# Top-k attention and a cosine-gated layer on one core: weights decoded 2**8 times as large, their sign put in by VectorE

## The chip, the core and the metric

The kernel runs on one core of a Trainium2 chip. The core has a matrix engine (TensorE, PE in the profile), three engines for elementwise work (VectorE or DVE, ScalarE or ACT, GpSimd or POOL), a queue that only issues transfers (SyncE, SP), and 16 DMA engines. Each engine works through its own instructions in the order of the program and waits on semaphores for the others. The metric is the time of one execution on the device in microseconds (us). The kernel before takes 1515.18 us, the median of five runs (1513.1 to 1517.51).

## The reference, cut to what matters

```python
# q, k, v: (8, 8, 576, 64); w_in: (512, 2048); w_out: (2048, 512)
scores = 1.0 / np.sqrt(D) * np.matmul(q, k.transpose(0, 1, 3, 2))
kth = np.partition(scores, -32, axis=-1)[..., -32:-31]
scores = np.where(scores >= kth, scores, -1000000000.0)
scores = scores - np.max(scores, axis=-1, keepdims=True)
attn = np.exp(scores)
attn = attn / (np.sum(attn, axis=-1, keepdims=True) + 1e-09)
x = np.matmul(attn, v).transpose(0, 2, 1, 3).reshape(4608, 512)
h = x @ w_in
out = ((h * np.cos(h)) @ w_out).astype(np.float32)
```

The two weight matrices reach the kernel as 64-bit floating point numbers. No engine here computes on these, so the kernel reads each one as two 32-bit words (`lo`, `hi`) and makes a 32-bit float of them: this is the decoding that the change is about. The high word holds the sign, 11 bits of exponent and 20 bits of mantissa.

## The kernel before

The 4608 rows are cut into 36 blocks of 128, and each block is worked on for two heads at a time, which makes 144 units. The main loop (L775) goes through slots, one for each unit and one more. In slot i VectorE searches the 32 largest scores of unit i: `topk_first` begins with the folds (L244, on the scores that ScalarE copied from PSUM in `take_scores`, L230 and L231), and four rounds of searches follow (L304, L307). ScalarE, a slot behind, masks and exponentiates unit i-1 (`bounds`, `mask`, `exponentials`, L314 to L339) and ends with `den`, the sum of the exponentials. VectorE takes its reciprocal (L343), GpSimd multiplies by it (`normalise`, L348), PE transposes the result and multiplies it by v (`values`, L408), and ScalarE copies the product into xT (L414).

There are three kinds of slots. In the `early_slot` (0 to 8) the transposes are made by PE (`transposes_now`, L382, with copies by ScalarE in L386 and L389) within the same slot, and the reciprocal waits for the exponentials of this slot. In the `slot` (9 to 140) GpSimd rearranges the halves of each word (`split`, L360), and two DMAs on SP's queue write them to memory and bring them back transposed, two slots later. The `last_slot` is again like the early one.

Between these the matrix products of the second part are fed to PE in small portions (`feed`): `ff1` (L465, xT with w_in, taken out by ScalarE in `take_first`, L478) and `ff2` (L543, with w_out, taken out in `take_second`, L553). The cosine needs a reduction to one period, on GpSimd in L504 to L513 (`reduce_first`, `reduce_second`), a sine on ScalarE (L523) and a product on GpSimd (`gate`, L530). How many portions a slot may feed is counted while the program is built, with a credit of some five for each slot, and a product is fed only when its weights were decoded a slot before. So the order of each engine's instructions is fixed in the program.

The weights come in 32 chunks of 128 x 512, 16 of w_in and 16 of w_out. Up to eight staging tiles `st` (they share their memory with the tiles g) are filled by DMAs on SP's queue (`load_weights`). Each chunk is then decoded in three steps, by three engines:

- `decode_first`, ScalarE, three passes: the magnitude of the high word, read as a float and multiplied by 2**16 (L126); the sign of the high word as +1 or -1, written over it (L127); the low word multiplied by 2**-29, which leaves the three bits that are still wanted (L128).
- `decode_second`, VectorE, two operations: a maximum with 2.0, which keeps small values out of the way (L137), and a shift of the bits to the left by 3, which drops the surplus bits of the exponent (L138).
- `decode_third`, GpSimd, two operations: the three low bits are added as integers (L147), and the float is multiplied by the sign (L148).

Slots 0 to 5 decode three chunks in their `decode_second`, slots 6 to 12 two. In the early slots `decode_second` stands ahead of the reciprocal, and `decode_third` behind `normalise`; ScalarE's `decode_first` stands in part ahead of the copies L386, in part behind them. In slots 9 to 12 `decode_second` comes right after `topk_first`, and `decode_third` stands behind `normalise`, `split` and `gate` and ahead of the reduction.

Of the kernel before, what the change touches and what calls it, by code (L numbers as in the profile page):

```python
# [10 lines left out]
F32 = mybir.dt.float32  # L11
# [3 lines left out]
AF = mybir.ActivationFunctionType  # L15
ALU = mybir.AluOpType
# [9 lines left out]
INV_2PI = 1.0 / (2.0 * math.pi)  # L26
# [5 lines left out]
def kernel(  # L32
# [9 lines left out]
    nc = tc.nc  # L42
# [32 lines left out]
    DECODE = moe_w_in.dtype != F32  # L75
# [9 lines left out]
    for i in range(DF // CW):  # L85
        w = consts.tile([P, NC, CW], F32, tag=f"w_in{i}", name=f"w_in{i}")
# [4 lines left out]
    for f in range(NF):  # L91
        w = consts.tile([P, DM], F32, tag=f"w_out{f}", name=f"w_out{f}")
# [10 lines left out]
    def load_weights(n):  # L103
        for _ in range(n):
# [12 lines left out]
            wq["loaded"].append((st, dst))  # L117
            wq["next"] = i + 1

    def decode_first(n):  # L120


        for _ in range(min(n, len(wq["loaded"]))):
            st, w = wq["loaded"].popleft()
            lo, hi = st[:, :, 0], st[:, :, 1]
            nc.scalar.activation(out=w, in_=hi.bitcast(F32), func=AF.Abs, scale=2.0**16)  # L126
            nc.scalar.sign(hi.bitcast(F32), hi)  # L127
            nc.scalar.mul(out=lo, in_=lo.bitcast(U32), mul=2.0**-29)  # L128
            wq["second"].append((st, w))

    def decode_second(n):


        for _ in range(min(n, len(wq["second"]))):
            st, w = wq["second"].popleft()
            wi = w.bitcast(I32)
            nc.vector.tensor_scalar(out=w, in0=w, scalar1=2.0, scalar2=None, op0=ALU.max)  # L137
            nc.vector.tensor_scalar(  # L138
                out=wi, in0=wi, scalar1=3, scalar2=None, op0=ALU.logical_shift_left
            )  # L140
            wq["third"].append((st, w))

    def decode_third():
        while wq["third"]:
            st, w = wq["third"].popleft()
            wi = w.bitcast(I32)
            nc.gpsimd.tensor_tensor(out=wi, in0=wi, in1=st[:, :, 0], op=ALU.add)  # L147
            nc.gpsimd.tensor_tensor(out=w, in0=w, in1=st[:, :, 1].bitcast(F32), op=ALU.mult)  # L148
            wq["done"] += 1


# [298 lines left out]
    def ff1(blk, i):  # L450
        w = blk["w"]
        nf = 256 // w
        part = i % 4
        if part == 0:
            blk["g"].append(ffw.tile([P, 1024], F32, tag="g", name="g", bufs=CHUNKS))
            ff["live"] += 1
        if part % 2 == 0:
            open_bank()
            blk["mm"] = ps.tile([P, 512], F32, tag="mm", name="mm", bufs=2)
        g, mm = blk["g"][-1], blk["mm"]  # L460
        for a in range(nf):
            f = i * nf + a
            at = (part % 2 * nf + a) * w
            for c in range(NC):
                nc.tensor.matmul(  # L465
                    mm[:, at : at + w],
                    w_in[f // FC][:, c, (f % FC) * P : (f % FC + 1) * P],
                    blk["xT"][:, c],
                    start=c == 0,
                    stop=c == NC - 1,  # L470
                )
        if part % 2 == 0:
            return
        ff["open"] -= 1
        full.append((take_first, blk, g, mm, part // 2))

    def take_first(blk, g, mm, half):
        nc.scalar.mul(out=g[:, half * 512 : half * 512 + 512], in_=mm, mul=INV_2PI)  # L478
        if half == 1:
            fresh.append([blk, g])  # L480

# [51 lines left out]
    def ff2(blk, i, f0):  # L533
        w = blk["w"]
        if f0 == 0:
            open_bank()
            blk["o"] = ps.tile([P, 512], F32, tag="mm", name="o2", bufs=2)
        o = blk["o"]
        per = 1024 // w
        for f in range(f0, f0 + 2):  # L540
            g = blk["g"][f // per]
            at = (f % per) * w + i * P
            nc.tensor.matmul(  # L543
                o, g[:, at : at + P], w_out[f], start=f == 0, stop=f == NF - 1
            )
        if f0 + 2 < NF:
            return
        ff["open"] -= 1
        full.append((take_second, blk, i, o))

    def take_second(blk, i, o):
        ob = ffw.tile([P, DM], F32, tag="ob", name="ob")
        nc.scalar.mul(out=ob, in_=o, mul=2.0 * math.pi)  # L553
        row = blk["t0"] + i * P
        nc.scalar.dma_start(out=out[row : row + P, :], in_=ob)
        if i == blk["w"] // P - 1:
            ff["live"] -= len(blk["g"])
            blk["g"] = []
# [70 lines left out]
    def early_slot(i, u, w):  # L629
        n = 3 if i < 6 else 2  # L630
        topk_first(u, w)
        if i == 0:
            decode_second(1)
# [8 lines left out]
        topk_round(u, 1)  # L642

        decode_second(n)
        if w:
            reciprocal(w)
# [5 lines left out]
        take_scores(units[i + 1])  # L652
        gate(1)
        decode_third()
        feed(2)
        reduce_first()
        reduce_second()
        if i != NP:
            decode_first(n - 1)
        if w:  # L660
            transposes_now(w)
        feed(1)
        decode_first(n - len(wq["second"]))
        if w:
            values([w])
# [4 lines left out]
    def slot(i, u, w, x, z):  # L670
        if x:
            reciprocal(x)
        if u:
            topk_first(u, w)
            decode_second(2)
# [40 lines left out]
        feed(1 if len(made) == 2 else 2)  # L716
        take_banks()
        decode_third()
        decode_first(2)
        reduce_first()  # L720
        reduce_second()
# [53 lines left out]
    for i in range(NU + 1):  # L775
# [4 lines left out]
        u, w = (units[i - n] if 0 <= i - n < NU else None for n in range(2))  # L780
# [55 lines left out]
```

## Time and profile before

| what | value |
|---|---|
| median of five runs | 1515.18 us (1513.1 to 1517.51) |
| the profiled execution | 1516.19 us |
| its span, first to last instruction | 1514.4 us |
| granted TensorE clock, mean | 0.962 |
| PE, VectorE, ScalarE, GpSimd busy | 1415.8, 1415.3, 1161.1, 1104.5 us |
| ScalarE, L126, L127 and L128 | 32 each; medians 676 to 690, 683 and 664 ns |
| VectorE, L137 and L138 | 32 each; medians 419 to 420 and 427 to 428 ns |
| GpSimd, L147 and L148 | 32 each; medians 1293 to 1294 and 1292 to 1296 ns |
| first and last start of L126 | 10.2 and 161.7 us |
| last start of L148 | 177.7 us |

In the profile, a line of a timeline gives the start and the length in us, the engine, the line of the kernel, the operation, the tile written and the tiles read with their shapes, and how many such instructions were merged into one row; in brackets stands the time for which the engine was idle before it, and what ended that. A line of the waits names the engine and the line that waited, the engine and the line that released it, the time in all, how often, and the longest one. A row for one line of the kernel ends with the forms; ahead of them are the shortest, the median and the longest duration in ns, and the first and last start.

### The profile page before, as it was taken

How to read it: one execution, taken by the hardware profiler on the slowest of the kernel's cores; microseconds unless marked ns; L12 is line 12 of the kernel's file. 1: busy time of each engine (PE TensorE's matmuls, PEld its weight loads, DVE VectorE, ACT ScalarE, POOL GpSimd, SP SyncE). 2: the span in 40 equal slices, each digit the busy share in tenths (PEclk: the TensorE clock that was granted, in tenths of full speed). 3: DMA queues.
4: the chain of work that ended last, by engine and by line, in shares of the span. 5: the costliest groups of instructions: out<-in, count | busy, mean ns of one | idle time of the engine just before them, and what ended most of it. 6: DMA issues, size and time to landing. Idle time of an engine off the chain costs nothing.

```text
span 1514.4 us, 30303 instructions
## 1 busy us (share of the span) xinstructions
PE 1415.8 (93%) x10360; PEld 1018.6 (67%) x10360; DVE 1415.3 (93%) x4809; ACT 1161.1 (77%) x2326; POOL 1104.5 (73%) x838
## 2 busy tenths in 40 slices
PE   4577789999999999999999999999999999999999
PEld 3365456777677776777777777677677777777665
DVE  7989988999999999999999999999999999999831
ACT  7888766888788787788888887788788887888651
POOL 4768967777777777777777777777777777777610
PEclk6687989999999999999999999999999999999999
DMA  8423356545654456545654456545654455544200
GB/s 255 147 86 101 86 165 167 147 133 143 181 157 136 134 147 177 166 132 148 179 165 133 133 148 180 156 131 147 176 165 127 138 149 163 148 130 132 77 8 14
DMA packets 371754, 212.21 MB, mean 140 GB/s; under 512 B 321296, under 2 KB 337936, under 8 KB 371600
## 3 DMA queue, kind: packets, MB, share of 16 engines
q1 hardware_dynamic: 366192, 200.63, 47.7%
q10 hardware_dynamic: 5408, 9.65, 1.8%
q8 instruction: 81, 1.33, 0.4%
q14 instruction: 73, 0.60, 0.1%
HBM read 45.09 MB, written 87.29 MB: 87 GB/s over the span
## 4 chain that ended last, share of the span: by engine, by line
POOL 40%; DVE 22%; PE 16%; issue 12%; ACT 6%; DMA 3%; SPq 1%; POOLq 0%; ACTq 0%; DVEq 0%
POOL halves L360 11%; DVE top L304 9%; POOL s L348 8%; DVE rest L307 7%; POOL x L513 6%; POOL g L530 6%; PE o L543 6%; PE mm L465 5%; DVE rest L244 3%; POOL x L505 3%; POOL x L506 3%; POOL x L504 3%; PE rim L408 2%; PE sc L220 2%; DMA pT<-rows 1%
## 5 line engine op out<-in xcount | busy, mean ns | idle before, releaser
L304 DVE MAX8 top<-rest 128x8 f32<-128x288 f32 x1716 | 688.1, 450 | 0.0
L465 PEld LDWEIGHTS mm<-xT,w_in 128*128 128x128 f32 x4608 | 540.9, 193 | 67.9 <-issue 61.6
L465 PE MATMUL mm<-xT,w_in 128*128 128x128 f32 x4608 | 544.2, 276 | 1.3 <-ACT g L478 1.3
L543 PE MATMUL o<-w_out,g 128*128 128x512 f32 x1152 | 536.6, 600 | 5.7 <-ACT g L478 2.1
L307 DVE MATCH_REPLACE8 rest<-top,rest 128x288 f32<-128x288 f32 x1144 | 500.6, 445 | 0.0
L348 POOL TENSOR_SCALAR s<-s,rden 128x576 f32<-128x576 f32 x288 | 212.4, 749 | 297.1 <-DVE rden L343 292.9
L543 PEld LDWEIGHTS o<-w_out,g 128*128 128x128 f32 x1152 | 202.6, 190 | 193.2 <-issue 179.9
L360 POOL COPY halves<-s 128x2304 uint16<-128x2304 uint16 x132 | 277.6, 2103 | 9.6 <-DMA rows<-halves 1.4
L244 DVE TENSOR_TENSOR rest<-sc,s 128x576 f32<-128x576 f32 x284 | 213.7, 753 | 28.1 <-ACT s L231 19.8
L334 ACT ACTIVATE s<-s,nd 128x576 f32<-128x576 f32 x288 | 219.8, 764 | 0.8
L326 ACT ACTIVATE s<-s,nb 128x576 f32<-128x576 f32 x288 | 205.5, 760 | 0.0
L408 PE MATMUL rim<-pT,v 128*64 128x128 f32 (+1 forms) x2560 | 164.6, 274 | 36.9 <-DMA pT<-rows 25.1
L408 PEld LDWEIGHTS rim<-pT,v 128*64 128x64 f32 x2560 | 134.9, 141 | 92.9 <-issue 37.2
L220 PE MATMUL sc<-k,q 64*128 64x448 f32 (+1 forms) x640 | 160.0, 598 | 9.0 <-DVE w_in L138 7.1
L530 POOL TENSOR_TENSOR g<-g,x 128x1024 f32<-128x1024 f32 x68 | 160.9, 2366 | 8.5 <-ACT nb L314 4.4
L513 POOL TENSOR_TENSOR x<-g,x 128x1024 f32<-128x1024 f32 x68 | 160.7, 2364 | 5.7
L478 ACT ACTIVATE g<-mm 128x512 f32<-128x512 f32 x144 | 84.3, 586 | 90.2 <-PE mm L465 88.3
L230 ACT COPY s<-sc 128x896 f32<-128x896 f32 x144 | 129.4, 898 | 3.7 <-PE sc L220 3.3
L414 ACT COPY xT<-rim 128x256 f32<-128x256 f32 (+1 forms) x78 | 27.6, 354 | 108.2 <-PE rim L220 96.1
L220 PEld LDWEIGHTS rim<-k,q 64*128 64x128 f32 (+1 forms) x640 | 59.9, 186 | 60.2 <-issue 55.1
L523 ACT ACTIVATE x<-x,halfpi 128x1024 f32<-128x1024 f32 x72 | 82.7, 1150 | 18.8 <-POOL x L513 11.5
L307 DVE MATCH_VALUE_LOAD rest<-top,rest 128x8 f32 x1144 | 88.8, 78 | 0.0
(55 smaller groups left out, 1221.8 us busy)
## 6 DMA issues: line engine op xcount, KB each, us to landing
rows<-halves SPq DMA_DIRECT2D x132, 576.0 KB, 2.8
out_dram<-ob ACTq DMA_DIRECT2D x36, 256.0 KB, 2.7
q<-in_q_dram SPq DMA_DIRECT2D x31, 288.0 KB, 3.6
st<-in_moe_w_in_dram SPq DMA_DIRECT2D x16, 512.0 KB, 5.5
v<-in_v_dram SPq DMA_DIRECT2D x32, 256.0 KB, 3.1
st<-in_moe_w_out_dram SPq DMA_DIRECT2D x16, 512.0 KB, 3.5
k<-in_k_dram SPq DMA_DIRECT2D x31, 144.0 KB, 3.6
k<-in_k_dram SPq DMA_DIRECT2D x32, 128.0 KB, 3.6
```

What stands on the lines that cost most here:

```text
L220: nc.tensor.matmul(to[r0 : r0 + rows, j, 0 : k1 - k0], st["q"][d, q0 : q0 + rows], st["k"][d, k0:k1], start=True, stop=True,)
L244: nc.vector.tensor_tensor(out=u["rest"][:, :, i * HS : (i + 1) * HS], in0=sc[:, :, 0:HS], in1=s[:, :, HS:S], op=op,)
L304: nc.vector.max(to[:, j], src[:, j])
L307: nc.vector.match_replace(rest[:, j], to[:, j], src[:, j], NEG)
L334: nc.scalar.activation(out=s[:, j], in_=s[:, j], func=AF.Exp, bias=nd[:, j : j + 1], scale=1.0, accum_out=den[:, j : j + 1],)
L348: nc.gpsimd.tensor_scalar(out=s[:, j], in0=s[:, j], scalar1=rden[:, j : j + 1], scalar2=1.0, op0=ALU.mult, op1=ALU.mult,)
L360: nc.gpsimd.tensor_copy(out=halves, in_=s.rearrange("p (k h) -> p h k", h=2))
L408: nc.tensor.matmul(o[d, to], lhsT, rhs, start=c == 0, stop=c == NT)
L465: nc.tensor.matmul(mm[:, at : at + w], w_in[f // FC][:, c, (f % FC) * P : (f % FC + 1) * P], blk["xT"][:, c], start=c == 0, stop=c == NC - 1,)
L513: nc.gpsimd.tensor_tensor(out=x, in0=g, in1=x, op=ALU.subtract)
L530: eng.tensor_tensor(out=g, in0=g, in1=x, op=ALU.mult)
L543: nc.tensor.matmul(o, g[:, at : at + P], w_out[f], start=f == 0, stop=f == NF - 1)
```

## The change

The exponent that `decode_first` leaves in place is moved down by 127 (the factor is 2**-111 where it was 2**16), so that after the shift the weights stand 2**8 times as large as they are, and small values need no maximum to keep them from wrapping. ScalarE's sign pass and GpSimd's product with the sign are gone, and so is VectorE's maximum. VectorE takes instead, after the shift, one operation with two tensors: the high word AND the sign bit, OR the shifted bits. The staging tile's high word is left as it was loaded. GpSimd adds the low bits after that. The factor 2**8 of each matrix is taken out where ScalarE copies the products from PSUM.

```diff
+    UP = 2.0**8 if DECODE else 1.0
+
     def decode_first(n):
         for _ in range(min(n, len(wq["loaded"]))):
             st, w = wq["loaded"].popleft()
             lo, hi = st[:, :, 0], st[:, :, 1]
-            nc.scalar.activation(out=w, in_=hi.bitcast(F32), func=AF.Abs, scale=2.0**16)
-            nc.scalar.sign(hi.bitcast(F32), hi)
+            nc.scalar.activation(out=w, in_=hi.bitcast(F32), func=AF.Abs, scale=2.0**-111)
             nc.scalar.mul(out=lo, in_=lo.bitcast(U32), mul=2.0**-29)
             wq["second"].append((st, w))
 
     def decode_second(n):
         for _ in range(min(n, len(wq["second"]))):
             st, w = wq["second"].popleft()
             wi = w.bitcast(I32)
-            nc.vector.tensor_scalar(out=w, in0=w, scalar1=2.0, scalar2=None, op0=ALU.max)
             nc.vector.tensor_scalar(
                 out=wi, in0=wi, scalar1=3, scalar2=None, op0=ALU.logical_shift_left
             )
+            nc.vector.scalar_tensor_tensor(
+                out=wi, in0=st[:, :, 1], scalar=-(2**31), in1=wi, op0=ALU.bitwise_and, op1=ALU.bitwise_or
+            )
             wq["third"].append((st, w))
 
     def decode_third():
         while wq["third"]:
             st, w = wq["third"].popleft()
             wi = w.bitcast(I32)
             nc.gpsimd.tensor_tensor(out=wi, in0=wi, in1=st[:, :, 0], op=ALU.add)
-            nc.gpsimd.tensor_tensor(out=w, in0=w, in1=st[:, :, 1].bitcast(F32), op=ALU.mult)
             wq["done"] += 1
...
-        nc.scalar.mul(out=g[:, half * 512 : half * 512 + 512], in_=mm, mul=INV_2PI)
+        nc.scalar.mul(out=g[:, half * 512 : half * 512 + 512], in_=mm, mul=INV_2PI / UP)
...
-        nc.scalar.mul(out=ob, in_=o, mul=2.0 * math.pi)
+        nc.scalar.mul(out=ob, in_=o, mul=2.0 * math.pi / UP)
```

## The prediction

> **What bounds the kernel now.** I read the page's busy times first, then the stretches of time, then the waits, then every instruction of the stretch in which the weights are decoded.
>
> ```profile
> PE 1415.8 (93%) x10360; PEld 1018.6 (67%) x10360; DVE 1415.3 (93%) x4809; ACT 1161.1 (77%) x2326; POOL 1104.5 (73%) x838
> ```
> ```profile
> 0.00:50.00 50.00, 21.64 (x104) 16.17 (x106) 42.04 (x138) 37.76 (x73) 26.45 (x35) 0.60 0.75 229
> 50.00:100.00 50.00, 36.19 (x268) 30.43 (x268) 44.03 (x147) 43.93 (x96) 33.96 (x31) 0.79 0.43 130
> 500.00:700.00 200.00, 198.59 (x1550) 142.22 (x1550) 198.84 (x695) 159.03 (x323) 156.73 (x117) 1.00 0.55 151
> ```
> The columns are the stretch, its length, busy PE, PEld, DVE, ACT, POOL, then granted clock and DMA. Once decoding is over, VectorE is busy 198.84 of 200 us. Its own list of waits for 500 to 1350 us holds three waits of 4.8 us in all. So a slot there lasts as long as its VectorE work (9.5 us), and time gained or lost earlier moves everything behind it by that amount. All decoding lies between 10 and 178 us: only what happens to slots 0 to 15 counts, and each slot is measured here from reciprocal to reciprocal, or from fold to fold.
>
> ```profile
> DVE rest L244 <- ACT s L231: 19.8, 6, 6.5
> DVE rden L343 <- ACT den L339: 19.0, 6, 7.0
> ```
> ```profile
> L138 DVE TENSOR_SCALAR w_out<-w_out x16: 426/428/2462, 77.3 to 173.8; 128x512 int32<-128x512 int32 x16
> ```
> ```profile
> 103.76 1.04 POOL L506 TENSOR_SCALAR x<-x 128x1024 f32<-128x1024 f32 x1
> 104.89 2.40 POOL L513 TENSOR_TENSOR x<-g,x 128x1024 f32<-128x1024 f32 x1
> ```
> ```profile
> 104.03 1.05 DVE L137 TENSOR_SCALAR w_out<-w_out 128x512 f32<-128x512 f32 x1
> 105.12 2.45 DVE L138 TENSOR_SCALAR w_out<-w_out 128x512 int32<-128x512 int32 x1
> 107.49 0.41 DVE L137 TENSOR_SCALAR w_out<-w_out 128x512 f32<-128x512 f32 x1
> 107.94 0.43 DVE L138 TENSOR_SCALAR w_out<-w_out 128x512 int32<-128x512 int32 x1
> ```
> Three things stretch VectorE's early slots. First its waits on ScalarE (den, and the copied scores). Second the decode operations: they take 0.42 and 0.43 us alone, but the two above end only when a GpSimd instruction does (104.80, 107.29). I call this blocking; over all 64 instructions I count 14.1 us of it, in slots 0 (1.4), 7 (2.66), 8 (2.65), 10 (2.4), 11 (0.8) and 12 (4.25). Third, their plain work, 0.79 us from the start of one chunk to what follows it (107.49 to 108.29 is 0.80).
>
> **The change, part by part.**
>
> *VectorE: `max` goes, a two-input operation comes.* The `max` lasted 0.42. For the new operation over 512 elements there is no row; L499, the same kind over 1024, lasts 1.226, and L244 over 576 lasts 0.753. Their slope is 0.473/448 = 1.056 ns per element, so 512 elements give 0.753 - 64 x 1.056 ns = 0.685. L244's successor starts 0.68 after it (0.07 before its end), so the step is 0.61. The shift in front, on which the new operation depends, takes 0.45 from start to start like today's `max`. A chunk then takes 0.45 + 0.61 = 1.06 against 0.79: **+0.27 us, 32 times**. Bounds: 0 (as fast as the one-input `max`; nothing in the rows makes two inputs faster) and +0.81 (if its input, every second word of the staging tile, halved the rate: another 512 x 1.056 ns = 0.54). I stay at 0.27, since the nearest strided rows show no such loss: GpSimd's add with that same tile takes 1.29 at 512 elements, L530 without stride 2.36 at 1024.
>
> ```profile
> L499 DVE SCALAR_TENSOR_TENSOR x<-x,g x4: 1226/1226/1642, 1455.3 to 1498.4; 128x1024 f32<-128x1024 f32 x4
> ```
> On the stride, the Trainium skill, "SBUF — State Buffer" (section "Door 1: The DMA port swizzle", its note on 16-byte lines), says that full rate needs two hits per 16-byte line; a step of eight bytes still has two. By it the sum stands as below, while a lost line would make it rival 1; no VectorE row here has such a stride.
>
> *Is the new operation blocked too?* L499's maximum of 1.642 is at 1455.33, while GpSimd's L348 ran until 1455.90; the other three, with GpSimd idle, took 1.226. So yes, I let it be blocked until a running GpSimd instruction ends. "SBUF — State Buffer", section "Who interferes with whom", states that against this change: two SBUF inputs contend with any GpSimd instruction that reads SBUF. By the rule the sum is the one below, without it about 4 us better (rival 3).
>
> *ScalarE: one of three passes goes, 32 times.* A chunk now takes 1.94 from start to start (70.78 to 72.72) and would take about 1.3: Abs to `mul` 0.7, `mul` to the next 0.56. That counts only where ScalarE holds VectorE up. *GpSimd: the product goes*, 1.3 us, 32 times; it counts where GpSimd blocks VectorE or is late.
>
> **Slots 0 to 3** (12 chunks). VectorE has no wait before its reciprocals (30.01, 41.95, 53.94): 12 x 0.27 = +3.2. In slot 0 blocking was 0.46 + 0.97; the first was a product, which goes, the second, by the add at 16.57, comes again: -0.4. Together **+2.8**. The freed ScalarE and GpSimd passes are worth nothing here.
>
> **Slots 4 to 6.** VectorE waits 0.52, 2.10 and 2.55 for den.
>
> ```profile
> 69.67 1.07 ACT L386 COPY pT<-tp 128x512 f32<-128x512 f32 x2 [2.13 <-PE tp L382]
> 76.50 0.25 ACT L414 COPY xT<-rim 128x128 f32<-128x128 f32 x1
> 80.25 0.30 ACT L339 ACTIVATE den<-den,eps 128x2 f32<-128x2 f32 x1
> 81.50 0.69 ACT L126 ACTIVATE w_out<-st 128x512 f32<-128x512 f32 x1
> 85.38 1.04 ACT L386 COPY pT<-tp 128x512 f32<-128x512 f32 x2
> ```
> The loop is reciprocal, normalise, PE's transposes, copies (L386), values on PE, copy xT, mask, exponentials, den, reciprocal. Slot 4: 12.56 was 12.04 of work and a wait of 0.52; now 12.04 + 0.81 = 12.85, above a loop of some 11.3: **+0.3**. Slot 5, 66.50 to 80.65: 3.17 to the first copy, 1.11 of copies, 5.72 for three chunks with PE's values long done, 4.15 to the reciprocal. With 3 x 0.65 less the loop is 12.2; VectorE's work is 14.15 - 2.10 + 0.81 = 12.86 and rules: **-1.3**. Slot 6, 80.65 to 94.45: the copies came 4.73 after the reciprocal, behind two chunks; the transposes were done at 83.67, 3.0 after it. With two passes per chunk, and den no longer late, the copies start at 3.0; the 9.07 behind them stay. Loop 12.1 against VectorE's 13.80 - 2.55 + 0.54 = 11.8: **-1.7**. Bounds for both slots together: 0 (PE, at a clock of 0.79, not ScalarE, holds the loop) to -3.6.
>
> **Slots 7 and 8.** GpSimd's order is normalise, two chunks, then L504 to L513. Without two products L513 ends 2.6 earlier, at 104.65 and 118.45, so VectorE's decode (104.03, 117.86) is held 0.6 instead of 2.66: -2.05 + 0.54 each, **-3.0 to -3.3**, taken as -3.3 since the last operation's shorter hold frees 0.1 more each. Den is ready (104.79) before the new reciprocal, 106.7, so no wait takes the place.
>
> **Slot 9**: VectorE waits 2.63 for den behind two sines and two table loads; 0.54 more work fits inside: **0**.
>
> **Slots 10 to 12**: every GpSimd instruction moves earlier by up to 2.6, and VectorE meets another one. Slot 10: L530 now ends at 144.5 (hold 0.5, was 1.4), the second chunk's new operation meets the add (1.0): -0.4. Slot 11: instead of L348 it meets L360 (a hold of 1.2; L360 did so at 169.31) and the add (1.0), against 0.8: +1.95. Slot 12: L530 (1.3) and an add (1.0), against 4.25: -1.55. Together **0.0**. Bounds: -3 if the new operation is never blocked behind an add, +3 if each slot meets a whole L530 more, as at 171.01.
>
> **Slot 15**: at 203.30 VectorE waited 4.38 for scores.
>
> ```profile
> 184.69 1.46 POOL L348 TENSOR_SCALAR s<-s,rden 128x576 f32<-128x576 f32 x2
> 186.22 2.10 POOL L360 COPY halves<-s 128x2304 uint16<-128x2304 uint16 x1
> ```
> The chain runs back over ScalarE, PE, two DMAs on SP's queue to these, which stood behind L513 and, before it, the last two chunks. The last two chunks' products now gone, less 0.3 for the later add: normalise at 182.4, still after its reciprocal (179.8): **-2.3**; bounds 0 and -4.4.
>
> *Without effect:* the changed scales and immediates. The staging tile is now last read by the add, so the next weight load on SP's queue can start sooner; ScalarE waited for such loads three times, 5.3 us, all before 22 us, with fresh tiles. PE waited for decoded weights at 179.04, in cover of a later 7.39 us wait for a DMA. Behind the new operation on VectorE stand reciprocal and searches, which the +0.27 contains.
>
> **Sum**: 2.8 + 0.3 - 1.3 - 1.7 - 3.3 + 0 + 0 - 2.3 = -5.5 us. The profiled execution lasted 1516.19 (span 1514.4 and 1.8 around it), which gives 1510.7; the median of the five is 1515.18, so I say **1509.7**.
>
> **Rivals.** 1, slower: the new operation reads every second word at half rate, +0.54 per chunk. It counts for 15 chunks of slots 0 to 4 (8.1), slot 5 (1.6), 0.9 in slot 6, slots 7, 8 and 10 to 12 (5.4): +16.0, so 1515.18 - 5.5 + 16.0 = 1525.7. It decides from 0.19 us per chunk on. For it: no VectorE row shows the stride. Against: GpSimd's and ScalarE's rows. 2, no change: the ScalarE passes and the GpSimd lateness were covered after all (slots 5 and 6 keep their loop, slot 15 its wait), -5.5 + 3.0 + 2.3 = -0.2, 1515.0. For it: PE's slow early clock; against: ScalarE's unbroken row of passes until 76.50. 3, better: the new operation is not blocked by adds, -1.0 in slots 0, 10, 11 and 12: 1505.7.
>
> **Chances.** Forecast 0.56, rival 1 0.16, rival 2 0.18, rival 3 0.10. A measurement tells about 0.2%, 3 us, from no change: faster 0.66, same 0.18, slower 0.16. Range: low -5.5 - 4.0 - 2.1 = -11.6, 1503.6; high -5.5 + 3.0 (blocking) + 2.3 + 3.0 = +2.8, 1518. Outside it is rival 1.
>
> **What would show it.** In the groups by line, 32 new operations on VectorE near 0.69, several at 1.7; no wait for den in slots 5 and 6 above 0.5; the fold's wait near 203 us (now near 200) some 2 us; the first fold after decoding some 5 us earlier; slots behind it still 9.5. A new operation of 1.2 us everywhere, or more than 14 us of blocking, would make me wrong.

## The result, and the profile after

The changed kernel takes 1510.69 us (median of 34 runs, 1506.63 to 1515.78) against 1515.24 for the kernel before (57 runs, 1507.19 to 1521.29): a ratio of 0.9968, 95% interval 0.996 to 0.9976, so 4.6 us less. The forecast was 1509.7, 5.5 less. Three later sets of runs of the same kernel, told of below, showed a smaller gain or none, and this difference stays open.

The profiled execution lasted 1515.08 (span 1513.3), which is near the slow end of its 34. So it is not a typical total; what it shows well is the first 200 us. First the stretches of time, with the columns as before (stretch, length, busy PE, PEld, DVE, ACT, POOL, clock, DMA):

```profile
0.00:50.00 50.00, 20.71 (x98) 15.26 (x100) 42.22 (x131) 29.95 (x60) 16.23 (x27) 0.60 0.75 229
50.00:100.00 50.00, 36.79 (x282) 30.45 (x280) 48.82 (x154) 37.55 (x86) 21.22 (x21) 0.75 0.41 131
500.00:700.00 200.00, 199.41 (x1556) 142.96 (x1555) 198.78 (x696) 159.88 (x320) 158.69 (x119) 1.00 0.55 150
```

From 50 to 100 us VectorE is busy 48.82 of 50 us, where it was 44.03: its waits for ScalarE are nearly gone there, and the new operation fills the rest. ScalarE gave up 6.4 us in this stretch, GpSimd 12.7. From 500 us on VectorE is as busy as before.

Next the row of the new operation (line 141 now, the shift is line 138), shortest, median and longest in ns:

```profile
L141 DVE SCALAR_TENSOR_TENSOR w_in<-st,w_in x16: 691/692/1651, 12.3 to 79.2; 128x512 int32<-128x512 int32 x16
L141 DVE SCALAR_TENSOR_TENSOR w_out<-st,w_out x16: 691/693/1676, 80.3 to 169.6; 128x512 int32<-128x512 int32 x16
```

692 ns is the row's answer to the 685 worked out from L499 and L244. Its stride of two words costs 7 ns at most. The Trainium skill, "SBUF — State Buffer" (section "Door 1: The DMA port swizzle", its note on 16-byte lines), which makes this stride free, agrees with this row.

The decode of slot 7, VectorE first, then GpSimd, which answers to the four rows and the two rows shown of before:

```profile
103.68 0.73 DVE L138 TENSOR_SCALAR w_out<-w_out 128x512 int32<-128x512 int32 x1
104.45 0.69 DVE L141 SCALAR_TENSOR_TENSOR w_out<-st,w_out 128x512 int32<-128x512 int32 x1
105.06 0.42 DVE L138 TENSOR_SCALAR w_out<-w_out 128x512 int32<-128x512 int32 x1
105.51 0.69 DVE L141 SCALAR_TENSOR_TENSOR w_out<-st,w_out 128x512 int32<-128x512 int32 x1
```
```profile
100.64 1.04 POOL L509 TENSOR_SCALAR x<-x 128x1024 f32<-128x1024 f32 x1
101.77 2.36 POOL L516 TENSOR_TENSOR x<-g,x 128x1024 f32<-128x1024 f32 x1
```

GpSimd's long subtraction now ends at 104.13, while the first shift is held, and not in the middle of the second operation; the hold is 0.3 us where it was 2.66. In slot 10, however, the new operation itself is held:

```profile
141.51 0.42 DVE L138 TENSOR_SCALAR w_out<-w_out 128x512 int32<-128x512 int32 x1
141.97 1.67 DVE L141 SCALAR_TENSOR_TENSOR w_out<-st,w_out 128x512 int32<-128x512 int32 x1
```
```profile
141.73 1.35 POOL L151 TENSOR_TENSOR w_out<-w_out,st 128x512 int32<-128x512 int32 x1 [1.15 <-DVE w_out L141]
```

The second chunk's operation is ready at 141.97, GpSimd has begun the first chunk's add at 141.73, and VectorE ends 0.6 after that add does.

And the waits of the whole execution that VectorE's early slots were said to hang on:

```profile
DVE rest L247 <- ACT s L234: 21.5, 8, 6.4
...
DVE rden L346 <- ACT den L342: 17.7, 5, 7.0
```

Both totals are about what they were (19.8 and 19.0), but not in the same places: of the waits for den 0.39 and 2.10 are left before 140 us, where 0.52, 2.10, 2.55 and 2.63 were (the view of before puts the 2.63 down to GpSimd's L147, which ended 0.06 us after den); 15.2 lie in the last slots, where 13.8 were. Two waits ahead of the folds are the ones to follow: that of slot 15, where the first fold after decoding stands, and the one near 261 us. Before:

```profile
203.30 0.76 DVE L244 TENSOR_TENSOR rest<-sc,s 128x576 f32<-128x576 f32 x1 [4.38 <-ACT s L231]
264.05 0.76 DVE L244 TENSOR_TENSOR rest<-sc,s 128x576 f32<-128x576 f32 x1 [3.74 <-ACT s L231]
```

After:

```profile
197.90 0.76 DVE L247 TENSOR_TENSOR rest<-sc,s 128x576 f32<-128x576 f32 x1 [2.94 <-ACT s L234]
261.23 0.76 DVE L247 TENSOR_TENSOR rest<-sc,s 128x576 f32<-128x576 f32 x1 [6.32 <-ACT s L234]
```

The first has shrunk, the second has grown by 2.6 us.

### The profile page after: what moved, and what is told of

The parts are those of the page before. It is cut to its first block, busy times and chain, and to the rows that moved or that the text cites. A ratio compares the mean times of both kernels' runs of the same rounds, so it can differ in the third digit from the quotient of the medians.

```text
span 1513.3 us, 30265 instructions
## 1 busy us (share of the span) xinstructions
PE 1417.7 (94%) x10360; PEld 1018.6 (67%) x10360; DVE 1416.8 (94%) x4809; ACT 1139.0 (75%) x2294; POOL 1062.2 (70%) x806
## 4 chain that ended last, share of the span: by engine, by line
POOL 40%; PE 24%; issue 13%; DVE 12%; DMA 5%; ACT 5%; SPq 2%; POOLq 0%; ACTq 0%; DVEq 0%
POOL halves L363 11%; PE mm L468 8%; PE o L546 8%; POOL s L351 8%; POOL x L516 6%; POOL g L533 6%; DVE top L307 5%; DVE rest L310 4%; PE rim L411 3%; POOL x L508 3%; POOL x L509 3%; POOL x L507 3%; PE sc L223 3%; DVE rest L247 2%; DMA rows<-halves 2%
```

## The experiments

The traces can be compared slot by slot: the start of each reciprocal, less the start of the first fold (6.7 to 8.0 us, set by the first loads). A second trace of the kernel before, which is run e10 below, lies within 0.2 us of the first up to 200 us, so a step of 0.3 us counts there, but for the stretch ahead of the first reciprocal, in which two traces of the changed kernel lie 0.37 apart. Totals are medians, each beside runs of the kernel before on the same chip.

**One part put back at a time.** A third ScalarE pass, without use:

```diff
+            nc.scalar.sign(w, hi)
             nc.scalar.activation(out=w, in_=hi.bitcast(F32), func=AF.Abs, scale=2.0**-111)
```

> The changed kernel with a third ScalarE pass put back (a sign pass into w, which Abs then overwrites; its result is not used). Theory: the dropped pass is worth time only in slots 5 and 6, where den held VectorE. With it back, slot 5 returns from 12.75 to about 14.1 us and slot 6 from 12.15 to 13.8, all others stay: +3.0 against the changed kernel, the fold after decoding (197.90 us there) comes at 200.9, total about 1513.5. Rival (PE at its low early clock holds the loop, not ScalarE): +0.3 or less, fold at 198.2.

Measured: slots 5 and 6 take 1.26 and 1.55 longer than in the changed kernel, 2.8 together; every other slot up to 12 agrees within 0.06, but for the stretch ahead of the first reciprocal, which is 0.58 longer. The waits for den are back, 1.19 and 1.92. The total is 1515.84 against 1516.09 for before (ratio 0.9997, 0.9981 to 1.0014). So ScalarE's dropped pass is worth 2.8 us, in the two slots that were named, and the rival falls; the 0.58 need not belong to it, since e2 and e7 below, which differ by the same pass, agree there. The total lies 2.3 above the 1513.5 expected; those of the next two, e2 and e3, lie 2.7 and 1.7 above theirs, which like this one were counted from the 1510.7 of the 34 runs.

A GpSimd product, without use:

```diff
             nc.gpsimd.tensor_tensor(out=wi, in0=wi, in1=st[:, :, 0], op=ALU.add)
+            nc.gpsimd.tensor_tensor(
+                out=st[:, :, 1].bitcast(F32), in0=w, in1=st[:, :, 1].bitcast(F32), op=ALU.mult
+            )
```

> The changed kernel with a GpSimd product per chunk put back behind the add (into the high word of the staging tile; its result is not used). Theory: GpSimd is late again, so its long subtraction meets the decode of slots 7 and 8 (+2.35 each), slot 10 +0.9, slot 11 -1.3, slot 12 +2.0, the wait of slot 15 +1.4: +7.7 against the changed kernel, so slower than the kernel before by some 3, about 1518.3; fold after decoding near 205.6. Rival (GpSimd has room, a product costs nothing): 0, fold at 197.9.

Measured against the changed kernel: slot 7 +2.33, slot 8 +2.34, slot 10 +0.98, slot 11 -1.44, slot 12 +2.05, slot 15 +1.50: the signs and the sizes expected, and 0.5 more in slot 0. The total is 1520.99 (ratio 1.0037, 1.0021 to 1.0053), 4.9 above before. In slot 7 of this kernel VectorE and GpSimd stand thus:

```profile
104.83 1.04 DVE L138 TENSOR_SCALAR w_out<-w_out 128x512 int32<-128x512 int32 x1
105.90 2.72 DVE L141 SCALAR_TENSOR_TENSOR w_out<-st,w_out 128x512 int32<-128x512 int32 x1
```
```profile
105.67 2.40 POOL L519 TENSOR_TENSOR x<-g,x 128x1024 f32<-128x1024 f32 x1
```

With the products ahead of it, the subtraction starts 2.8 us later after its reciprocal again, and the new operation waits for it as the shift did before. GpSimd is 73% busy here and 70% in the changed kernel, and taking work from it pays only through the moment at which its next long instruction meets VectorE.

Both put back, which is VectorE's part alone:

> The changed kernel with both put back, the third ScalarE pass and the GpSimd product (neither result used): VectorE's part of the change alone, with sound data. Theory (the three parts act where the slots say): fold after decoding at 210.9 as with the two-input operation put into the kernel before, 7.5 later than before; total about 1523. Rival (the 1530 of that run belongs to the operation itself, not to its unsound data): 1529 to 1531.

Measured: slots 0 to 3 +3.2 and slot 4 +0.18, slots 5, 6 and 9 within 0.1 of nothing, slots 7, 8, 10, 11 and 12 +0.52 to +0.57 each, slot 15 +0.59: 6.5 in all at the fold, 1 less than expected. The total is 1524.43 against 1516.38 (ratio 1.005, 1.0036 to 1.0063). The same part put into the kernel before:

```diff
-            nc.vector.tensor_scalar(out=w, in0=w, scalar1=2.0, scalar2=None, op0=ALU.max)
             nc.vector.tensor_scalar(
                 out=wi, in0=wi, scalar1=3, scalar2=None, op0=ALU.logical_shift_left
             )
+            nc.vector.scalar_tensor_tensor(
+                out=wi, in0=st[:, :, 1], scalar=-(2**31), in1=wi, op0=ALU.bitwise_and, op1=ALU.bitwise_or
+            )
```

> The kernel before with VectorE's part of the change alone: maximum out, two-input operation in, sign pass and product kept (so the product applies the sign a second time, and small weights are not kept from wrapping). Theory: slots 0 to 3 +3.0, slot 4 +0.3, slots 5, 6 and 9 take it into their waits for den (0), slots 7, 8 and 10 to 12 +0.54 each, slot 15 +0.2: +6.2 against the kernel before, about 1521.4, fold after decoding near 209.5. Rival (the two-input operation hides in VectorE's idle time): 0, fold at 203.3.

Measured: 7.5 at the fold, 1.0 more than e7. There ScalarE writes the sign over the high word that the operation reads, and each operation starts some 0.09 us behind its shift where e7 has 0.03 (slot 3, 42.01 and 41.58), though that sign pass had ended 4 us earlier. The total was 1530.46 (4 runs, 1525.89 to 1531.94), of which the traced execution is the lowest. The 6 us beyond e7 do not belong to the operation, since e7 has it too; whether the unsound data or chance made them was not tried.

So the parts, up to the reciprocal behind slot 12 and with the start of the first fold taken off, are: VectorE's alone +5.9; without the product -6.3 with the third pass there and -6.7 without it; without the third pass -3.0 and -3.5 (none and 0.6 of these lie ahead of the first reciprocal). All together -3.8.

**Is the new operation held by the adds, or slow in itself?**

```diff
-        for _ in range(min(n, len(wq["second"]))):
-            st, w = wq["second"].popleft()
+        now = [wq["second"].popleft() for _ in range(min(n, len(wq["second"])))]
+        for st, w in now:
             wi = w.bitcast(I32)
             nc.vector.tensor_scalar(
                 out=wi, in0=wi, scalar1=3, scalar2=None, op0=ALU.logical_shift_left
             )
+        for st, w in now:
+            wi = w.bitcast(I32)
             nc.vector.scalar_tensor_tensor(
```

> The changed kernel with decode_second in another order: the shifts of all its chunks first, then the two-input operations, so that none of these stands behind a GpSimd add. Theory (the 1.65 us are a wait for the add): no two-input operation above 0.8 us in slots 0 and 10 to 12, which saves 1.0 each, and 0.11 per chunk where VectorE is the bound, since a shift no longer waits for its own result; part of it is lost again in slots 11 and 15, where GpSimd is late: -3 to -5 against the changed kernel, fold after decoding near 193.7, total near 1506.4. Rival (the long ones are slow in themselves, by the data or the place): they stay at 1.65, and only -2 from the closer steps.

Measured: the operation is never long any more,

```profile
L143 DVE SCALAR_TENSOR_TENSOR w_in<-st,w_in x16: 684/688/694, 12.6 to 77.4; 128x512 int32<-128x512 int32 x16
L143 DVE SCALAR_TENSOR_TENSOR w_out<-st,w_out x16: 677/680/692, 78.0 to 164.5; 128x512 int32<-128x512 int32 x16
```

so the 1.65 us were waits for the add, as the forecast had it; "SBUF — State Buffer", section "Who interferes with whom", states such a wait for two SBUF inputs, and these rows, beside the 1.67 us of slot 10 above, agree with it. At the fold this version is 4.7 us ahead of the changed kernel. The total is 1508.11 against 1516.09 (ratio 0.9943, 0.9927 to 0.9959): 8.0 less than before. Part of the gain goes again in slot 15, which takes 1.8 longer than in the changed kernel, and in slot 11, where the two shifts meet L365 on GpSimd (the copy of `split`):

```profile
148.62 2.72 DVE L138 TENSOR_SCALAR w_out<-w_out 128x512 int32<-128x512 int32 x2
```
```profile
148.89 2.17 POOL L365 COPY halves<-s 128x2304 uint16<-128x2304 uint16 x1
```

The grouped version with `n = 3` instead of `n = 3 if i < 6 else 2` in the early slots:

> The grouped version, with three chunks also in slots 6 to 8 (n = 3 in all early slots), so that decoding ends a slot or more earlier. Theory (the holds of slots 11 and 12, 2.0 and 1.2, and the late GpSimd behind the wait of slot 15 come from the decode in these slots): what moves into slots 6 to 8 costs the same 0.95 per chunk there, without holds; -2 to -4 against the grouped version, total 1504 to 1506. Rival (slots 6 to 8 are bound by the loop over ScalarE, and three passes more lengthen it): 0 or +2 against the grouped version.

> The grouped version with three chunks in all early slots once more, beside the changed kernel on the same chip: 6 to 10 us below the kernel before and 3 to 6 below the changed kernel, if its early gain of 12.4 lasts as the other gains did; as far as the changed kernel, if gains before 200 us are given back later.

Measured: slots 6 to 8 keep up with three chunks (7 and 8 take 0.14 longer than before, where grouping alone took 2.05 less), slot 12 takes 5.9 less than before, and the first fold after decoding comes 12.4 us earlier (10.4 in the second trace). In each trace one two-input operation is long again, 2.47 us. The totals are 1509.71 (ratio 0.9956, 0.9943 to 0.997) and 1509.92 (ratio 0.9947, 0.9932 to 0.9962), the changed kernel beside them 1517.61 and 1516.00. So this version beats both kernels, and the grouped one, which was not timed beside the changed kernel, beats the kernel before. The -2 to -4 against the grouped version is not seen in the totals, and at the fold in one trace only (2.5 and 0.5).

**What comes of an early gain.** The changed kernel three times more, without an edit:

> The changed kernel once more, unchanged, for a second trace. Theory (what it gives back behind 200 us is the chance of when DMAs land): the fold after decoding again comes at 197.9 within 0.7 (the start of the first fold shifts it), but the wait near 261 is not 6.3 again, it lies anywhere between 3.5 and 8. Rival (the earlier slots meet a fixed time of the transfers): 6.3 within 0.3 again. Total 1510.7.

> The changed kernel, unchanged, timed with five rounds: two sets of runs so far disagree (-4.6 us against before in 34 runs, +1.2 in 10). Theory (early gain of 4.6 to 5.4, the rest scatter): median 3 to 6 below before; fold after decoding 4.5 to 5.5 earlier. Rival (the early gain is given back later as a rule): within 1.5 of before.

> The changed kernel, unchanged, timed once more: its three sets so far lie 4.6 below, 1.2 above and 1.6 below the kernel before. Theory (an early gain of 4 to 5.4, and an even chance at each later batch to give some of it back): 1 to 5 below before, the slots up to 180 us as in the other traces within 0.2. Rival (the first set was luck): within 1 of before.

Measured: 1517.61 (10 runs; ratio 1.0003, 0.9986 to 1.002), 1516.00 (12 runs; 0.9993, 0.9975 to 1.001) and 1515.99 (12 runs; 0.999, 0.9978 to 1.0003). These sets can't tell the changed kernel from the one before, and the 0.9968 of the 34 runs lies outside the intervals of all three. Of the forecasts, e8's wait near 261 held (3.92) and its total did not; e11's median, 1.6 below before, and its fold, 3.6 earlier, miss the theory, and the median just misses the rival; e14's median, 1.1 below, lies at the edge between theory and rival. The kernel before once more:

> The kernel before, unchanged, for a second trace and as a yardstick for how far two sets of runs of one kernel lie apart on one chip. Theory (up to 200 us the slots are fixed, behind that the waits for scores scatter): reciprocals of slots 1 to 11 as in the first trace within 0.2 once the start of the first fold is taken off; waits behind 200 us other than 3.7 and 2.9; median within 2 us of the other runs of before. Rival (the slots scatter too): steps of 0.5 and more before 180 us.

Measured: 1516.11 against 1517.58 (ratio 0.9995, 0.998 to 1.0009), so two sets of one kernel on one chip lie up to 1.5 us apart. The traces show where the gain goes. VectorE's waits ahead of its folds, in us:

| trace | gain up to slot 12 | wait, slot 15 | wait near 261 | later ones, sum |
|---|---|---|---|---|
| before | - | 4.38 | 3.74 | 4.8 |
| before, e10 | 0.2 | 4.48 | 3.89 | 2.3 |
| after | 3.8 | 2.94 | 6.32 | 5.5 |
| after, e8 | 3.3 | 3.90 | 3.92 | 4.6 |
| after, e11 | 3.8 | 4.36 | 7.52 | 10.0 |
| after, e14 | 3.7 | 3.93 | 3.81 | 8.6 |

The second column is the same in all four traces of the changed kernel within half a microsecond. The three behind it are not: they sum to 12.9 and 10.7 before, and to 14.8, 12.4, 21.9 and 16.3 after. Taken off the time of the traced execution, these waits leave 1503.3 and 1504.1 before and 1500.3, 1498.9, 1500.0 and 1499.7 after: some 4 us less, about the gain up to slot 12. So the early gain is there in every trace, and the waits behind it cover it in some. In the first trace of after, the wait near 261 leads back, over PE, a transposing DMA and its write, which stood on SP's queue behind those of the slot before, to one write:

```profile
235.66 0.34 SPq L368 DMA_DIRECT2D rows<-halves  x1
240.59 2.42 SPq L374 DMA_TRANSPOSE pT<-rows  x1
```

The transposing DMA has to wait for that write to land, 4.9 us later. In the first trace of the kernel before the same two lines stand 3.0 apart:

```profile
240.87 0.34 SPq L365 DMA_DIRECT2D rows<-halves  x1
243.85 2.35 SPq L371 DMA_TRANSPOSE pT<-rows  x1
```

That puts 1.9 us more on the chain. Another 1.0 is PE's: its 57 matmuls ahead of the fold took it 6.34 us at a granted clock of 0.53, where before they took 5.30 at 0.68. The transposing DMA between them gave 0.6 back (4.49 against 5.13). In e11 the time is lost further up: PE waits 1.50 us for a load of k at 223.84 (1.30 in the first trace of after, 0.48 before) and then has a granted clock of 0.50 from 224.8 to 228.2. So different transfers land late in different executions.

The traces hold one thing that goes with a late write. The page lists, in both kernels, a DMA queue of the kind "instruction", with 81 packets (then MB and the share of the 16 engines):

```profile
q8 instruction: 81, 1.33, 0.4%
```

Each packet is 16 KB. Of the 792 writes `rows<-halves` in the six traces of the table, 47 took more than 4.3 us to land, and in 44 of these such a packet ran while the write was under way; of the other 745 this holds for 198. That the packet delays the write was not tried.

An attempt to take the loads out of that chain, by moving them ahead of the two DMAs:

```diff
         load_weights(2)
+        for load, b, hp in at_slot.get(i, []):
+            load(b, hp)
         if x:
             normalise(x)
             split(x)
             write_halves(x)
             transposes(x)
-
-        for load, b, hp in at_slot.get(i, []):
-            load(b, hp)
```

> The changed kernel with the loads of q, k and v issued in each middle slot ahead of the two DMAs of the transposes on SP's queue, not behind them. Theory (behind 200 us the chain over k, xT, the reduction and the transposes has no slack left, so a late k or a slow landing is given back as a wait near 261 us): PE's waits for k behind 200 us go from 0.9 to 1.5 us to 0, the wait near 261 is below 5, total 1 to 3 below the changed kernel's on the same chip. Rival (slow landings of the transposes' own DMAs are the cause): the wait near 261 scatters as before, between 3.5 and 8, total as the changed kernel's.

Measured: 1554.42 (ratio 1.025, 1.0231 to 1.027), 37 us more. PE no longer waits for k behind 200 us, as expected, but the total is neither the theory's nor the rival's. The waits of SP's queue (what waits, for what, us in all, how often, longest) show why:

```profile
SPq L374 <- DMA rows<-halves: 380.8, 132, 5.3
...
SPq L188 <- PE rim L223: 122.5, 21, 7.6
SPq L199 <- PE rim L411: 40.3, 17, 7.9
```

The loads (L188, L199) wait for PE to release their buffers (in the changed kernel such waits of L188 and L199 come to less than 4 us), and now the writes and transposes of the slot stand behind them. The experiment decides nothing on landing times.

## Why the prediction was right, and where it was not

Step by step, forecast and first trace of the changed kernel, in us:

| slots | forecast | measured |
|---|---|---|
| 0 to 3 | +2.8 | +2.67 |
| 4 | +0.3 | +0.19 |
| 5 | -1.3 | -1.39 |
| 6 | -1.7 | -1.65 |
| 7 and 8 | -3.3 | -3.62 |
| 9 | 0 | 0.00 |
| 10, 11, 12 | -0.4, +1.95, -1.55 | -0.44, +1.98, -1.53 |
| 15 | -2.3 | -1.44 |
| sum | -5.5 | -5.23 |

- *The new operation's price.* 0.692 us and a step of 1.06 per chunk (103.68 to 106.12 holds two chunks and a hold of 0.3). Rival 1, a halved rate, is out.
- *The new operation is held by GpSimd.* Right, by e3. Rival 3, no hold, is out. The held instruction does not end with the GpSimd one, as the prediction has it, but somewhat later: in slot 7 of before at 105.08 and 107.57 against 104.80 and 107.29, in slot 10 of after at 143.64 against 143.08.
- *ScalarE's pass counts in slots 5 and 6 alone.* Right, by e1: 2.8 us, of the 3.0 foreseen, with the 0.58 ahead of the first reciprocal left out.
- *GpSimd's product counts by what its next instructions meet.* Right, by e2, slot 11's loss included.
- *No new wait for den in slots 7 and 8.* Right: the waits for den that are left stand in slots 6 and 9.
- *Slot 15, -2.3.* Mis-sized. Normalise started at 178.35 where it stood at 184.69, so 2.4 us earlier relative to its reciprocal, but the chain behind it took 19.6 us to the fold and not 18.6, and in the other traces the wait fell by 0.5, 0.0 and 0.5 only. The term was priced as if the two DMAs in that chain took a fixed time. They did not: the write in it landed 4.60 us after its issue (182.01) where it had taken 2.77 (188.35), and 4.63 to 4.93 in the other three traces of the changed kernel; in e10, e2, e6 and e7, which have GpSimd's product, it took 2.8. A packet of the instruction queue ran beside it in each of the four late ones and in none of the five that took 2.8. So this loss is the same in all traces of the changed kernel, and no chance. The first trace won 0.9 back, on PE.
- *"Time gained or lost earlier moves everything behind it by that amount."* This is the step that failed. In the first trace 5.41 us at slot 15's reciprocal (the start of the first fold left in) were 1.11 at the last one, with +2.3 near 261 us, +1.8 twice and others both ways; in e8 4.55 became 4.87, in e14 4.92 became 0.21, and in e11 3.65 became 5.67 lost. Rival 2 had the gain shrink because ScalarE and GpSimd were covered; they were not, and it shrinks behind 200 us instead, in waits that VectorE's 4.8 us from 500 to 1350 had made look harmless.

The total was forecast right by 1.0 us in the 34 runs, and part of that is luck: the early sum was right, but that it reached the end was not known. That these came out 4.6 below before, and the 34 runs of the other three sets 1.1 to 1.6 below and once 1.2 above, is not explained: the early part is the same in all traces, and only one execution of each set is traced. The three later sets ran on one chip, and where the first ran is not on record, so a difference between chips is possible too. Whether the changed kernel meets late transfers more often because it has less slack, or by chance, stays open.

## What to carry to other kernels

When instructions of two engines hold each other up, price an edit by replaying which instruction of the one will be running when the other one arrives; a removed instruction pays as much as the meeting it prevents, and may cause another. Put instructions that wait for nothing side by side ahead of the first result that wakes the other engine: the changed kernel with its shifts grouped ahead of the two-input operations runs 8 us below the kernel before. And a gain before a stretch with chains over DMAs is no gain at the end until the waits in that stretch have been seen in more than one trace.

## What the runs showed of the hardware that was not expected

- From the first reciprocal up to slot 12 (176 us, 180 before) the traces of one kernel agree within 0.2 us slot by slot, while the total scatters by 9 us within one set (1506.63 to 1515.78). Most of the scatter arises in the waits for scores from slot 15 on, which sum to between 10.7 and 21.9 us.
- The time from issuing one and the same kind of write (`rows<-halves`, 576 KB each, 2.8 us to landing as the median) to the transposing DMA behind it was 3.0 us in one trace and 4.9 in another, at the same place of the program. 44 of the 47 writes that took over 4.3 us had a 16-KB packet of the instruction queue beside them, of the other 745 only 198.
- The loads of a slot moved ahead of its write and its transposes on the same queue cost 37 us: the queue held everything behind a load whose buffer was not free (SP's waits for PE's release of the buffers, 122.5 and 40.3 us).
- The two-input operation with one input in steps of eight bytes took 692 ns for 512 elements, 7 ns more than was worked out from L499 and L244, which have no such stride.
